# Chunk 0 of the first batch in halves of the heads, query chunk 2 behind the first products, w1 ahead of w2

## The chip, the cores and the metric

The kernel runs on one core of a Trainium2 chip. The metric is the device time of one execution in microseconds (us), of which the median of several runs is taken. Five engines work at once, each through its own list of instructions in order: PE (TensorE: matrix products and transposes; its weight loads are shown apart as PEld), DVE (VectorE), ACT (ScalarE), POOL (GpSimd) and SP (SyncE), the last two here mostly to issue transfers. PE writes to PSUM, an accumulation memory that DVE and ACT read; everything else lies in SBUF.

## What is computed

A linear attention with cosine weights feeds a multiplicative feed-forward layer. There are 8 batches of 8 heads, 576 positions and 64 features:

```
r = relu(x);  phi(x) = [r * cos(theta), r * sin(theta)]          # 128 features, for q and k
kv = phi(k)^T @ v;   z = sum over positions of phi(k)
attn = (phi(q) @ kv) / (phi(q) @ z + 1e-6)
x = attn as (4608 tokens, 512)
out = ((x @ w1) * (x @ w2)) @ w3 @ w_out                          # w1, w2: 512 x 1024
```

The kernel computes `w3 @ w_out` once and applies it as one matrix, `w34b`. It works in bf16, with sums in fp32.

## The kernel before, in words

**Tiles and stages.** The positions of a batch are cut into five chunks, four of 128 and one of 64. For each chunk `features` writes phi of q or k: the cosine half on DVE (L264), the sine half on ACT (L268), with a DVE variant (L271) for four heads of the very first chunk. `kv_first` (for batch 0) and `kv_chunk` (for the others) sum kv and z on PE. `q_tr` and `q_tr_halves` transpose phi(q) of a chunk on PE, one 128x128 transpose for each of the 8 heads, into a PSUM tile `pst`, and copy it to `qpT` (L344 in two halves with two PSUM tiles, L332 on DVE or L333 on ACT as one copy). `num` (L359) makes 8 products of 65 columns for a chunk, numerator and denominator, into a two-bank PSUM tile, four heads in each bank. Its `normalize` adds 1e-6 to the denominators (L375), inverts them (L376) and multiplies (L377) into the block `xblk`. `x_tr` transposes that block with four PE transposes (L411) into a `pst` tile and copies them to `xT` (L413), 512 tokens wide.

The feed-forward layer runs over 9 tiles of 512 tokens (`ffn_groups`). For tile 0, with four chunks that come one after another, the first products (L456) are made in pieces: half a tile, and of that quarters of 128 tokens, so that they can begin when chunk 0 is there. `multiply` copies x @ w1 out of PSUM on ACT (L461) and multiplies on DVE (L462). The products with `w34b` come last (L526).

**What sets the order.** The order is written out by hand (`manual_schedule`): every engine gets its instructions in the order in which the Python code calls them, and waits by semaphores that the framework sets. What depends on what in PSUM is tracked by bank: a second access to a bank from another engine waits for the first, also where the columns differ. `ffn_groups` is a generator that yields between groups of products, and the main loop calls at each yield what `at(slot, ...)` has put there, so attention work stands between the products. `pst` tiles come from the pool `ps_tr` with two buffers, taken in turn: the third tile can be written when the copies of the first have ended.

**Around the change.** Before the loop, the start-up is written out: kv of batch 0, the features and transposes of query chunks 0 to 2, `num(0, 0)`, the marker that releases further loads on POOL (`other_loads`, which waits for `xblk` of chunk 0), the features of chunk 3, `x_tr(0, 0)`, `num(0, 1)`, and the transposes of query chunk 2 with their ACT copy. `idle_mms` are products of zeros that no one reads. Slot 1, behind the first quarter of products, holds `x_tr(0, 1)`, the transposes of query chunk 3 and `num(0, 2)`. Slot 3 holds `x_tr(0, 2)` and `num(0, 3)`.

In the first quarter of tile 0 the products alternate between the two weights:

```
for quarter in range(2):
    for i in range(2):
        for ps, w in ((a, w1b), (b, w2b)):
            products(ps[:, ds(256 * i + 128 * quarter, 128)], w, i, ...)
        if half == 0 and quarter == 0 and i == 0:
            yield
```

The first yield is slot 0, which is empty before the change.

Of the kernel before, what the change touches and what calls it, by code (L numbers as in the profile page):

```python
# [11 lines left out]
BF16 = mybir.dt.bfloat16  # L12
I32 = mybir.dt.int32
ALU = mybir.AluOpType
ACTF = mybir.ActivationFunctionType

P = 128
H, S, D = 8, 576, 64
# [5 lines left out]
def columns_of(b, c):  # L24


    if b % 2 == 0:
        return 128 * c
    return 0 if c == 4 else 64 + 128 * c
# [39 lines left out]
def kernel(  # L69
# [11 lines left out]
    nc = tc.nc  # L81
# [53 lines left out]
    w1b = const.tile([P, 4, DFF], BF16, name="w1b")  # L135
    w2b = const.tile([P, 4, DFF], BF16, name="w2b")
# [108 lines left out]
    feat = {}  # L245
# [8 lines left out]
    def att_of(b):  # L254
        if b not in att:
            att[b] = {"qpT": phi.tile([P, H, S], BF16, name="qpT"), "x": {}}
        return att[b]

    def features(b, dst, src, c, cos=True, sin=True, scalar_heads=H):

        R = ROWS[c]
        at = c if b == 0 else NCH + c
        if cos:
            nc.vector.tensor_scalar(out=dst[:R, c, :, 0:D], in0=src[:R, :, c, :], scalar1=0.0,  # L264
                                    scalar2=cosv[:R, at:at + 1], op0=ALU.max, op1=ALU.mult)
        if sin:
            n = scalar_heads
            nc.scalar.activation(out=dst[:R, c, 0:n, D:F], in_=src[:R, 0:n, c, :], func=ACTF.Relu,  # L268
                                 scale=sinv[:R, at:at + 1], bias=0.0)
            if n < H:  # L270
                nc.vector.tensor_scalar(out=dst[:R, c, n:H, D:F], in0=src[:R, n:H, c, :],  # L271
                                        scalar1=0.0, scalar2=sinv[:R, at:at + 1],
                                        op0=ALU.max, op1=ALU.mult)
# [51 lines left out]
    def q_tr(b, c, evac=True):  # L325
        R = ROWS[c]
        qp = feat[b][1]
        pst = ps_tr.tile([P, 8, 128], BF16, name="pst")
        for h in range(H):
            nc.tensor.transpose(pst[:, h, :], qp[:, c, h, :], identb[:])  # L330
        dst, src = att_of(b)["qpT"][:, :, ds(columns_of(b, c), R)], pst[:, :, 0:R]
        on_vector = lambda: nc.vector.tensor_copy(out=dst, in_=src)  # L332
        on_scalar = lambda: nc.scalar.copy(out=dst, in_=src)  # L333
        if evac:
            on_vector()
        return on_vector, on_scalar

    def q_tr_halves(b, c):

        for half in range(2):  # L340
            pst = ps_tr.tile([P, 8, 128], BF16, name="pst")
            for i in range(4):
                nc.tensor.transpose(pst[:, i, :], feat[b][1][:, c, 4 * half + i, :], identb[:])
            nc.vector.tensor_copy(out=att_of(b)["qpT"][:, ts(half, 4), ds(columns_of(b, c), 128)],  # L344
                                  in_=pst[:, 0:4, :])

    def num(b, c, chain=True, in_two=False):
        rows = out_rows(b, c)
        R = ROWS[c]
        at = columns_of(b, c) - rows.start  # L350
        qpT, kvs = att[b]["qpT"], att[b]["kvs"]
        if b == 0 and c == 0:
            nt = ps_first.tile([P, 2, 512], FP32, name="pfirst")
        else:
            pool = more_att[0] if more_att and order_of(b).index(c) % 2 == 0 else ps_att
            nt = None if in_two else pool.tile([P, 2, 512], FP32, name="pnum")
        banks = [ffn_tile(), ffn_tile()] if in_two else [nt[:, g, :] for g in range(2)]
        for h in range(H):
            nc.tensor.matmul(banks[h // 4][:, ds((h % 4) * 65, 65)], lhsT=qpT[:, h, ds(at, 128)],  # L359
                             rhs=kvs[:, h, :], start=True, stop=True)  # L360
        if b < 2:
            rows, R = slice(0, P), P
        if in_two:
            parts = [(slice(g, g + 1), t[rows, 0:260].rearrange("p (g h e) -> p g h e", g=1, e=65))
                     for g, t in enumerate(banks)]
        else:
            parts = [(slice(0, 2), nt[rows, :, 0:260].rearrange("p g (h e) -> p g h e", e=65))]
        xblk = sm.tile([P, 2, 4, D], BF16, name="xblk", bufs=4)
        att[b]["x"][c] = xblk

        def normalize():
            den = sm.tile([P, 2, 4], FP32, name="den")
            for g, n4 in parts:
                G = g.stop - g.start
                nc.vector.tensor_scalar_add(out=den[rows, g], in0=n4[:, :, :, 64], scalar1=1e-6)  # L375
                nc.vector.reciprocal(out=den[rows, g], in_=den[rows, g])  # L376
                nc.vector.tensor_tensor(out=xblk[rows, g], in0=n4[:, :, :, 0:D],  # L377
                                        in1=den[rows, g].unsqueeze(3).to_broadcast([R, G, 4, D]),
                                        op=ALU.mult)

        if chain:
            normalize()
        return normalize
# [9 lines left out]
    xT = {}  # L393

    def x_tr(b, c, by_vector=False):
        R, rows = ROWS[c], out_rows(b, c)
        xblk = att[b]["x"].pop(c)
        xf = xblk[:].rearrange("p g h d -> p (g h d)")
        if b % 2 == 0:
            slot = S * b + 128 * c  # L400
        else:
            slot = S * b + (0 if c == 4 else 64 + 128 * c)
        t, o = divmod(slot, 512)
        if t not in xT:
            xT[t] = xtp.tile([P, 4, 512], BF16, name="xT")
        if b >= 2 or (b, c) in ((0, 4), (1, 3)):
            nc.sync.dma_start_transpose(out=xT[t][:, :, ds(o, R)], in_=xf[rows])
            return
        pst = ps_tr.tile([P, 8, 128], BF16, name="pst")
        for kc in range(4):  # L410
            nc.tensor.transpose(pst[:, kc, :], xf[:, ts(kc, 128)], identb[:])  # L411
        copy = nc.vector.tensor_copy if by_vector else nc.scalar.copy
        copy(out=xT[t][:, :, ds(o, R)], in_=pst[:, 0:4, rows])  # L413
# [36 lines left out]
    def ffn_groups(t):  # L450
# [15 lines left out]
        def on_half(half):  # L466

            if half == 1 and t == 0:
                banks = [(ffn_tile(), ffn_tile()) for _ in range(2)]
                for quarter in range(2):  # L470
                    for pair, (a, b) in enumerate(banks):
                        for i in range(2):
                            for ps, w in ((a, w1b), (b, w2b)):
                                products(ps[:, ds(256 * i + 128 * quarter, 128)], w, 2 * pair + i,
                                         ds(256 + 128 * quarter, 128))
                        if quarter == 1:
                            multiply(a, b, pair, half)
                        if quarter == 0 or pair == 1:
                            yield
                return  # L480
            for pair in range(2):
                a, b = ffn_tile(), ffn_tile()
                if pair == 0 and t == 0:
                    for quarter in range(2):
                        for i in range(2):
                            for ps, w in ((a, w1b), (b, w2b)):
                                products(ps[:, ds(256 * i + 128 * quarter, 128)], w, i,
                                         ds(256 * half + 128 * quarter, 128))
                            if half == 0 and quarter == 0 and i == 0:
                                yield  # L490
                        if quarter == 0:
                            yield
                else:
                    for ps, w in ((a, w1b), (b, w2b)):
                        for i in range(2):
                            products(ps[:, ts(i, 256)], w, 2 * pair + i, ts(half, 256))
                        if w is w1b and (t == 1 or half == 0):
                            yield
                multiply(a, b, pair, half)
                yield  # L500
# [52 lines left out]
    def at(s, *calls):  # L553
        slots[s] += calls
# [42 lines left out]
    num(0, 0)  # L597
    q_tr(0, 1, evac=False)[1]()
    other_loads(att[0]["x"][0][:, 0, 0, 0:1])
    features(0, q0f, q0, 3, sin=False)  # L600
    features(0, q0f, q0, 3, cos=False)
    idle_mms(2)
    x_tr(0, 0, by_vector=True)
    num(0, 1)
    q_tr(0, 2, evac=False)[1]()
    ps_ffn = []
    for stack in first:
        stack.close()
# [2 lines left out]
                                                     space=bass.MemoryType.PSUM)))  # L611


    at(1, lambda: x_tr(0, 1, by_vector=True), lambda: q_tr(0, 3, evac=False)[1](), lambda: num(0, 2))
    at(3, lambda: x_tr(0, 2), lambda: num(0, 3))
    at(5, lambda: x_tr(0, 3))
# [74 lines left out]
```

## Time and profile before

| what | value |
|---|---|
| median of 5 runs | 249.3 us (249.09 to 249.71) |
| the profiled execution, its own time | 249.5 us |
| span of its profile | 247.7 us |
| granted TensorE clock, mean | 0.996 |
| busy: PE, DVE, ACT, POOL | 97%, 55%, 53%, 38% of the span |
| first products of tile 0 (L456) | 16.11 us |
| first products of its second quarter | 18.08 us |

The profile shows one execution. Its parts are the busy time of each engine, who waited for whom, the chain of work that ended last (followed back from the last instruction), and the timeline: one row for each group of equal instructions with its start, its duration, engine, line, operation, output and inputs, and, in brackets, the idle time of its engine before it and what ended that. Starts count from the beginning of the span. Matmuls overlap: the next starts before the one before has ended, so PE's pace is read from the starts.

### The profile page before, as it was taken

The page shows a single profiled execution, that of the slowest core. Times are in us where ns is not written, and L with a number is a line of the kernel's source. Part 1 is how long each engine was busy: PE and PEld are TensorE (multiplying, and loading weights), DVE is VectorE, ACT ScalarE, POOL GpSimd, SP SyncE. Part 2 cuts the span into 40 slices and gives each one's busy share as a digit, 9 for nine tenths or more (in the row PEclk, how much of TensorE's full clock was granted, in tenths as well). Part 3 has the DMA queues.
Part 4 walks back from the last instruction along what each step waited for, and adds up shares of the span by engine and source line. Part 5 has one row for each costly group of instructions (what it writes and reads, how often), then busy time and mean ns, then how long its engine had stood idle before and what let it go on. Part 6 is the DMA issues. An engine that isn't in the chain of part 4 may idle for free.

```text
span 247.7 us, 5041 instructions
## 1 busy us (share of the span) xinstructions
PE 241.5 (97%) x1872; PEld 130.4 (53%) x1872; DVE 136.5 (55%) x336; ACT 130.4 (53%) x266; POOL 93.2 (38%) x196
## 2 busy tenths in 40 slices
PE   8999999999999999999999999999999999999993
PEld 2479545566965445455544555455545544444442
DVE  7875652668967445656665575557554643403320
ACT  2676323767933973476448655754585234334322
POOL 7655342124412361217122622352231006969600
PEclk9999999999999999999999999999999999999998
DMA  6999999999989979999999999999995428898925
GB/s 196 177 194 199 201 207 205 198 185 174 155 141 154 163 117 152 126 142 95 170 175 166 128 159 149 173 155 112 170 124 111 88 42 247 263 292 276 294 51 127
DMA packets 84745, 41.22 MB, mean 166 GB/s; under 512 B 52337, under 2 KB 81265, under 8 KB 84721
## 3 DMA queue, kind: packets, MB, share of 16 engines
q0 software_dynamic: 35472, 27.20, 72.0%
q1 hardware_dynamic: 49088, 13.57, 36.4%
q8 instruction: 14, 0.23, 0.4%
q10 hardware_dynamic: 160, 0.13, 0.2%
q14 instruction: 11, 0.08, 0.1%
HBM read 38.80 MB, written 9.44 MB: 195 GB/s over the span
## 4 chain that ended last, share of the span: by engine, by line
PE 92%; DMA 3%; DVE 1%; issue 1%; POOL 1%; ACT 0%; ACTq 0%; POOLq 0%
PE ffnps L456 50%; PE ffnps L526 24%; PE ffnps L231 6%; PE pnum L359 4%; PE pnum L299 4%; DMA qs<-in_q_dram 3%; PE pst L219 1%; PE pst L330 1%; PE pst L411 1%; POOL vs L127 0%; PE ffnps L542 0%; ACT osb L544 0%; DVE xblk L377 0%; PE pfirst L359 0%; ACTq L441 0%
## 5 line engine op out<-in xcount | busy, mean ns | idle before, releaser
L456 PE MATMUL ffnps<-xT,w2b 128*128 128x512 bf16 (+2 forms) x344 | 75.5, 344 | 0.0
L456 PE MATMUL ffnps<-xT,w1b 128*128 128x512 bf16 (+2 forms) x344 | 75.5, 344 | 0.0
L513 DVE TENSOR_TENSOR abT<-asb,ffnps 128x512 bf16<-128x512 bf16 x64 | 43.9, 687 | 53.9 <-PE ffnps L456 52.0
L526 PE MATMUL ffnps<-w34b,abT 128*128 128x512 bf16 x280 | 65.0, 379 | 0.0
L509 ACT CAST asb<-ffnps 128x512 bf16<-128x512 f32 x64 | 37.4, 585 | 50.0 <-PE ffnps L456 45.2
L456 PEld LDWEIGHTS <-w2b 128*128 128x128 bf16 x344 | 31.0, 98 | 27.3
L456 PEld LDWEIGHTS <-w1b 128*128 128x128 bf16 x344 | 30.6, 98 | 26.1 <-issue 0.6
L561 POOL COPY seen<-mark 1x1 bf16<-1x1 bf16 x50 | 8.9, 177 | 85.9 <-ACT mark L559 85.8
L526 PEld LDWEIGHTS <-abT 128*128 128x128 bf16 x280 | 26.0, 98 | 27.9 <-DVE abT L513 0.2
L533 ACT COPY osb<-ffnps 128x512 f32<-128x512 f32 x35 | 20.5, 585 | 34.9 <-PE ffnps L526 34.8
L268 ACT ACTIVATE qp<-qs,sinv 128x512 bf16<-128x512 bf16 (+2 forms) x40 | 28.1, 714 | 2.0 <-DMA qs<-in_q_dram 2.0
L377 DVE TENSOR_TENSOR xblk<-pnum,den 128x512 bf16<-128x512 f32 (+1 forms) x37 | 25.6, 691 | 1.3
L291 POOL COPY va<-vs 128x512 bf16<-128x512 bf16 (+1 forms) x30 | 18.0, 631 | 21.5 <-DMA vs<-in_v_dram 21.1
L268 ACT ACTIVATE kp<-ks,sinv 128x512 bf16<-128x512 bf16 (+1 forms) x35 | 25.0, 718 | 1.0 <-DMA ks<-in_k_dram 1.0
L441 POOL DMA_DIRECT2D out_dram<-osb x42 | 22.1, 531 | 2.5 <-issue 2.1
L359 PEld LDWEIGHTS <-qpT 128*128 128x128 bf16 x320 | 15.4, 98 | 8.7 <-DVE qpT L344 0.6
L375 DVE TENSOR_SCALAR den<-pnum 128x8 f32<-128x8 f32 (+1 forms) x37 | 6.1, 164 | 22.6 <-PE pnum L359 22.5
L231 PE MATMUL ffnps<-woutb,w3T 128*128 128x512 bf16 x64 | 15.8, 380 | 0.0
L359 PE MATMUL pnum<-kvs,qpT 128*128 128x65 bf16 x296 | 15.8, 194 | 0.0
L264 DVE TENSOR_SCALAR qp<-qs,cosv 128x512 bf16<-128x512 bf16 (+1 forms) x40 | 15.3, 391 | 0.7 <-DMA qs<-in_q_dram 0.7
L299 PEld LDWEIGHTS <-kp 128*128 128x128 bf16 x280 | 11.4, 98 | 4.1
L264 DVE TENSOR_SCALAR kp<-ks,cosv 128x512 bf16<-128x512 bf16 (+1 forms) x35 | 12.9, 377 | 0.0
(86 smaller groups left out, 182.4 us busy)
## 6 DMA issues: line engine op xcount, KB each, us to landing
out_dram<-osb POOLq DMA_DIRECT2D x16, 256.0 KB, 4.5
out_dram<-osb POOLq DMA_DIRECT2D x24, 128.0 KB, 3.7
qs<-in_q_dram POOLq DMA_DIRECT2D x9, 256.0 KB, 7.3
ks<-in_k_dram POOLq DMA_DIRECT2D x7, 320.0 KB, 5.9
qs<-in_q_dram POOLq DMA_DIRECT2D x7, 320.0 KB, 6.1
vs<-in_v_dram POOLq DMA_DIRECT2D x7, 320.0 KB, 5.7
ks<-in_k_dram POOLq DMA_DIRECT2D x7, 256.0 KB, 7.0
vs<-in_v_dram POOLq DMA_DIRECT2D x7, 256.0 KB, 5.1
```

The costliest lines, as they stand in the source:

```text
L231: nc.tensor.matmul(acc[:, :], lhsT=w3T[:, lc, :], rhs=woutb[:, lc, :], start=(lc == 0), stop=(lc == 7))
L264: nc.vector.tensor_scalar(out=dst[:R, c, :, 0:D], in0=src[:R, :, c, :], scalar1=0.0, scalar2=cosv[:R, at:at + 1], op0=ALU.max, op1=ALU.mult)
L268: nc.scalar.activation(out=dst[:R, c, 0:n, D:F], in_=src[:R, 0:n, c, :], func=ACTF.Relu, scale=sinv[:R, at:at + 1], bias=0.0)
L299: nc.tensor.matmul(kvt[:, h // 4, ds((h % 4) * 65, 65)], lhsT=kp[:, c, h, :], rhs=va[:, c, h, 0:D + 1], start=(i == 0 and h % 4 == 0), sto ...
L359: nc.tensor.matmul(banks[h // 4][:, ds((h % 4) * 65, 65)], lhsT=qpT[:, h, ds(at, 128)], rhs=kvs[:, h, :], start=True, stop=True)
L377: nc.vector.tensor_tensor(out=xblk[rows, g], in0=n4[:, :, :, 0:D], in1=den[rows, g].unsqueeze(3).to_broadcast([R, G, 4, D]), op=ALU.mult)
L441: on.dma_start(out=rows[:, :, cols], in_=osb[64 * i:64 * i + rows.shape[0], :, cols])
L456: nc.tensor.matmul(out, lhsT=w[:, kc, ts(jc, 128)], rhs=x[:, kc, tok], start=(kc == 0), stop=(kc == 3))
L509: nc.scalar.copy(out=asb[:], in_=aT[:, :])
L513: nc.vector.tensor_mul(out=abT[:, jc, :], in0=asb[:], in1=bT[:, :])
L526: nc.tensor.matmul(ops[:, :], lhsT=abT[:, jc, ts(ms, 128)], rhs=w34b[:, jc, :], start=(jc == 0), stop=(jc == 7))
L533: nc.scalar.copy(out=osb[:, ms % 2, :], in_=ops[:, :])
```

## The change

Four things change, all in the start-up of batch 0 and in tile 0.

1. For chunk (0, 0), `normalize` multiplies in two halves of four heads, and `x_tr` makes two transposes and one copy of 128x256 for each half, both copies on DVE. One `pst` tile holds both halves.
2. The cosine features of chunk 3 on DVE are called behind `x_tr(0, 0)` instead of ahead of it; the sine features on ACT stay ahead.
3. The transposes of query chunk 2 move from ahead of the loop to slot 0. The new `q_tr_two` copies four heads on ACT and four on DVE, from one `pst` tile.
4. In the first pair of tile 0's half, the w1 products of both column groups come ahead of the w2 products, and slot 0 lies between them.

```
+    def q_tr_two(b, c):
+        pst = ps_tr.tile([P, 8, 128], BF16, name="pst")
+        for h in range(H):
+            nc.tensor.transpose(pst[:, h, :], feat[b][1][:, c, h, :], identb[:])
+        dst = att_of(b)["qpT"][:, :, ds(columns_of(b, c), 128)]
+        nc.scalar.copy(out=dst[:, 0:4], in_=pst[:, 0:4, :])
+        nc.vector.tensor_copy(out=dst[:, 4:8], in_=pst[:, 4:8, :])
...
-                nc.vector.tensor_tensor(out=xblk[rows, g], in0=n4[:, :, :, 0:D],
-                                        in1=den[rows, g].unsqueeze(3).to_broadcast([R, G, 4, D]),
-                                        op=ALU.mult)
+                for i in (range(G) if (b, c) == (0, 0) else [slice(0, G)]):
+                    i = slice(i, i + 1) if isinstance(i, int) else i
+                    part = slice(g.start + i.start, g.start + i.stop)
+                    nc.vector.tensor_tensor(
+                        out=xblk[rows, part], in0=n4[:, i, :, 0:D],
+                        in1=den[rows, part].unsqueeze(3).to_broadcast([R, i.stop - i.start, 4, D]),
+                        op=ALU.mult)
...
         pst = ps_tr.tile([P, 8, 128], BF16, name="pst")
+        if (b, c) == (0, 0):
+            for half in range(2):
+                for kc in range(2 * half, 2 * half + 2):
+                    nc.tensor.transpose(pst[:, kc, :], xf[:, ts(kc, 128)], identb[:])
+                nc.vector.tensor_copy(out=xT[t][:, ts(half, 2), ds(o, R)], in_=pst[:, ts(half, 2), rows])
+            return
...
                     for quarter in range(2):
-                        for i in range(2):
-                            for ps, w in ((a, w1b), (b, w2b)):
+                        for ps, w in ((a, w1b), (b, w2b)):
+                            for i in range(2):
                                 products(ps[:, ds(256 * i + 128 * quarter, 128)], w, i,
                                          ds(256 * half + 128 * quarter, 128))
-                            if half == 0 and quarter == 0 and i == 0:
+                            if half == 0 and quarter == 0 and w is w1b:
                                 yield
...
-    features(0, q0f, q0, 3, sin=False)
     features(0, q0f, q0, 3, cos=False)
     idle_mms(2)
-    x_tr(0, 0, by_vector=True)
+    x_tr(0, 0)
+    features(0, q0f, q0, 3, sin=False)
     num(0, 1)
-    q_tr(0, 2, evac=False)[1]()
...
+    at(0, lambda: q_tr_two(0, 2))
     at(1, lambda: x_tr(0, 1, by_vector=True), lambda: q_tr(0, 3, evac=False)[1](), lambda: num(0, 2))
```

## The prediction

> **What bounds the kernel now.** I read the page's first two parts, then who TensorE (PE) waited for, then the chain that ended last, and then the timeline of 14 to 18 us. Line numbers are those of the kernel before.
>
> From the page, the busy times:
>
> ```profile
> PE 241.5 (97%) x1872; PEld 130.4 (53%) x1872; DVE 136.5 (55%) x336; ACT 130.4 (53%) x266; POOL 93.2 (38%) x196
> ```
>
> Everything that the matrix engine waited for, over the whole span (total us, times, longest):
>
> ```profile
> PE unread L180 <- DVE zeros L156: 1.2, 1, 1.2
> PE pst L411 <- DVE xblk L377: 0.3, 1, 0.3
> PE pst L343 <- DVE qp L271: 0.3, 1, 0.3
> ```
>
> The reader is to see that PE is the bound, and that its last recorded idle time ends at 15.07 us, where the transposes of chunk 0 (L411) wait for the normalized block (L377). Behind it PE has work queued to 243 us, and waits for nothing that is tied to an absolute time, such as a load. So whatever the change gains or loses before the steady stream begins moves the whole rest and appears once, undiminished, in the time. The change touches 14 to 19 us alone, so the question is when the work behind it starts.
>
> The chain of waits in the window from 0 to 32 us (start, us, what):
>
> ```profile
> 14.32 0.70 DVE xblk L377
> ...
> 15.07 0.40 PE pst L411 x4
> 15.47 0.36 PE pnum L359 x8
> 15.83 0.45 PE pst L330 x8
> 16.28 0.89 PE ffnps L456 x16
> 17.17 0.28 PE pst L411 x4
> 17.45 0.53 PE pst L330 x8
> 17.98 0.26 PE pnum L359 x8
> 18.24 1.77 PE ffnps L456 x24
> ```
>
> From the timeline of 14 to 18 us (start, us, engine, line), the rows that the sum uses:
>
> ```profile
> 14.33 1.01 ACT L333 COPY qpT<-pst 128x1024 bf16<-128x1024 bf16 x1 [0.32 <-PE pst L330]
> ...
> 15.50 0.42 DVE L413 COPY xT<-pst 128x512 bf16<-128x512 bf16 x1 [0.23 <-PE pst L411]
> ...
> 15.87 0.17 DVE L375 TENSOR_SCALAR den<-pnum 128x8 f32<-128x8 f32 x1
> ...
> 16.31 0.69 DVE L377 TENSOR_TENSOR xblk<-pnum,den 128x512 bf16<-128x512 f32 x1
> 16.32 1.01 ACT L333 COPY qpT<-pst 128x1024 bf16<-128x1024 bf16 x1 [0.35 <-PE pst L330]
> ...
> 17.38 0.61 PE L330 MATMUL pst<-identb,qp 128*128 128x128 bf16 x8
> ...
> 18.08 0.39 PE L456 MATMUL ffnps<-xT,w1b 128*128 128x128 bf16 x4
> ```
>
> Two small waits are left in that stretch. The second L411 group issues at 17.06, 0.05 after chunk 1's block ends (16.31 + 0.69 = 17.00). The transposes of query chunk 3 issue at 17.38 and not at 17.28, because their PSUM buffer is that of query chunk 2, whose ScalarE (ACT) copy ends at 16.32 + 1.01 = 17.33. My mark is the row at 18.08, the first products of the second quarter: from there PE runs without a wait.
>
> **Prices.** From the starts of successive rows: a 128-column PE instruction issues every 0.055 us (L411 to L359 at 17.06, 17.38: 8 transposes 0.44, 8 products 0.45), a 65-column one every 0.033 (8 take 0.26), and a transpose ends 0.22 after it starts, so a pair takes 0.28. A signal needs 0.05 from VectorE (DVE) to PE (15.01 to 15.06), 0.03 from PE to DVE (15.47 to 15.50), 0.04 from PE to ACT, 0.03 from ACT to DVE (19.59 to 19.62). From the groups of DVE and then of ACT, kept apart by shape (mean ns in the last column but one):
>
> ```profile
> L377 DVE TENSOR_TENSOR xblk<-ffnps,den 128x256 bf16<-128x256 f32 x4 | 1.7, 424 | 0.1
> ...
> L221 DVE COPY w3T<-pst 128x1024 bf16<-128x1024 bf16 x8 | 5.5, 691 | 9.1 <-PE pst L219 9.1
> ...
> L413 ACT COPY xT<-pst 128x512 bf16<-128x512 bf16 x4 | 2.3, 576 | 1.9 <-PE pst L411 1.9
> ```
>
> A 128x256 DVE copy out of PSUM has no row. The 128x512 copy takes 0.42 and the 128x1024 one 0.69, so 256 elements cost 0.135 beside a fixed 0.15: 0.285. Bounds are 0.15 and 0.42.
>
> **Part 1: chunk 0 in halves.** The two normalize halves take 0.42 each, the second starting about 0.08 before the first ends (as L264 at 14.93 does behind L377): 14.32 to 14.74 and 14.66 to 15.08. So the first pair of transposes can issue at 14.79 instead of 15.07, a gain of 0.28. But both pairs write one PSUM tile, in one bank, and in the built program the second pair waits not only for the second half of the block but also for DVE's copy of the first pair. That makes a ladder: pair 14.79 to 15.07; copy 15.10 to 15.39; second pair 15.44 to 15.71; copy 15.74 to 16.02; PE hears of it at 16.07. Queued behind the waiting pair, in order, stand the 8 products of num(0,1) (their query columns are ready at 15.34 from ACT, so they could start at 15.39): they now issue from 15.55 to 15.82. Then come the first w1 products, of which two need only the first half of xT; the third waits until 16.07, and the other six issue by 16.41. Before, 16 products started at 16.11. The bounds on the copy shift 16.07 by -0.27 and +0.27.
>
> The cosine features of chunk 3 (L264) ran at 14.93 in DVE's idle time. They now stand behind the two xT copies, at about 15.94, and ahead of den(0,1), which starts at 16.22 and not at 15.87. Chunk 1's block is then ready at about 17.36 and its transposes issue at about 17.41 instead of 17.06. GpSimd's marker for the further loads waits for the first half alone and moves 0.27 earlier; no product waits for those loads, so I count nothing. SP gets no changed order.
>
> **Part 2: query chunk 2.** Its 8 transposes leave their place before the first products and go behind the w1 ones: issued 16.41 to 16.85, the last ending at 17.01. (Before: 15.67 to 16.28.) In the built program the DVE copy of heads 4 to 7 waits for ACT's copy of heads 0 to 3, since both read one bank. ACT: 17.05 to 17.63 (0.58). DVE: 17.66 to 18.08 (0.42). One ACT copy of both took 1.01, so the split saves nothing: 0.58 + 0.03 + 0.42 = 1.03. Behind that stand the transposes of query chunk 3, which need the same buffer: 18.08 + 0.05 = 18.13 instead of 17.38.
>
> The Trainium skill ("PSUM — Partial Sum Buffer", section "PSUM bank collisions raise a hardware error") says that two engines must be kept from one bank and quadrant at the same time, reads against reads included, so this order is a necessity and not a choice of the scheduler; by a sum without it, the two copies would lie side by side, 0.36 us earlier.
>
> **Part 3: w1 ahead of w2.** It is the same 16 products in another order, 0.45 per eight. Inside the first quarter it only gives the place for part 2. In the second quarter it lets ACT's first multiply copy (L461) start earlier, off PE's path. Cost 0, covered by PE's own queue; without that cover it could be worth 0.45 either way.
>
> **Sum.** PE's w2 products run from 16.85 to 17.30, chunk 1's transposes 17.41 to 17.63, then idle until 18.13; query chunk 3 to 18.57, num(0,2) to 18.83, and the second quarter begins at 18.83 instead of 18.08: **+0.75 us**. DVE's copy of chunk 1's xT (18.00 to 18.42) and all behind it are in time for that. Against the profiled execution's 249.5 us (span 247.7) this gives 250.25; the median of the five runs is 249.3, 0.2 lower, so for a median I say **250.1**.
>
> **Rivals.**
> A. Only one of the two bank waits costs its price. Without the wait of the second pair, num(0,1) starts at 15.39, w1 at 15.66, chunk 2's transposes end at 16.71, ACT ends at 17.33, DVE at 17.78: query chunk 3 at 17.83, +0.45. Without the wait between the copies, DVE's copy runs behind chunk 1's block, 17.30 to 17.72, ACT's to 17.63: 17.77, +0.39. In time: 249.7 to 249.75. For it: PE and DVE starts can be off by some hundredths. Against: both waits stand in the built program.
> B. Not slower: early start pays. If neither wait costs anything, chunk 3's transposes issue at 17.4 to 17.5, +0.1. If the ladder ends early enough (w1 products begun by 15.6, both copies of chunk 2 done before 17.2), PE loses all its idle time between 14.72 and 18.08: 0.35 before 15.07, 0.05 and 0.11 behind it, about 0.5: 248.8. The decision point is the end of chunk 2's copies against 17.33; I find it at 18.08, so 0.75 would have to be missing.
> C. More idle time lowers the granted clock. The row for 14.10 to 15.07 shows PE 0.62 us busy of 0.97 at a clock of 1.00, and only 240.0 to 247.7, with 4.1 us idle, shows 0.88. My gaps are 0.37 and 0.32. If one came all the same, the stretch of 3.4 us to 18.1 at half speed would add as much again: up to 253.5.
> D. The change does not do what it says: the order in the built program is that of the text, so only its waits decide, which is A and B.
>
> **How the numbers follow.** Chances: forecast 74%, its own range +0.5 to +1.0 by the copy's bounds (249.8 to 250.3); A 14%; B 8%, of which half is a real gain; C 4%. The range from 249.6 to 250.6 takes in A and a longer ladder, and leaves out B and C. Two kernels can be told apart from about 0.2%, 0.5 us. Faster by more: 4%, from B. Within: the rest of B and most of A, 16%. Slower by more: the forecast, some of A, and C, 80%.
>
> **What would show it.** In the profile after: the first transposes of chunk 0 at 14.8 (part 1's gain); the second pair near 15.44 and its copy ending near 16.0 (the ladder); den(0,1) near 16.2; ACT and DVE copies of chunk 2 one behind the other, ending near 18.1; a PE wait of about 0.3 to 0.5 before query chunk 3; the second quarter at 18.8. I am wrong if chunk 2's copies overlap, if half copies take much less than 0.28, or if PE has a wait further on that swallows the shift.

## The result, and the profile after

The changed kernel takes longer: median **250.62 us** over 54 runs (249.96 to 252.27), against 249.69 over 94 runs of the kernel before (249.09 to 252.31). The ratio is 1.0039, 95% interval 1.0031 to 1.0047, which is +0.97 us (0.77 to 1.17). The profiled execution took 250.12 us with a span of 248.3, against 249.5 and 247.7.

The loss is in the stretch that the change touches. Line numbers after the change: products L474 (before L456), transposes of chunk 0 in pairs L425 with their copies L426, those of the other chunks L429 and L431, `q_tr_two` L341 (transposes), L343 (ACT), L344 (DVE), `num` L367, normalize L383, L384, L388. In the experiments some of them shift by a line or two; with two tiles (e8, e3) `q_tr_two` has its transposes in L343 and both copies in L344. In both traces the loads of this execution come at slightly different times: q landed 0.44 us earlier after the change. So I do not compare bare starts, but count from one event that lies ahead of all the edits: DVE's start on the denominators of chunk 0, at 13.88 us before and 13.44 us after. To the first products of the second quarter it is 18.08 - 13.88 = 4.20 us before and 18.46 - 13.44 = 5.02 us after: **+0.82**. From there to the end of the span it is 229.62 and 229.84 (the spans are given to a tenth, so these two are good to 0.05).

Everything that PE waited for after the change (total us, times, longest):

```profile
PE unread L180 <- DVE zeros L156: 1.2, 1, 1.2
PE pst L425 <- DVE xT L426: 0.4, 1, 0.4
PE pst L429 <- DVE xblk L388: 0.2, 1, 0.2
PE pst L351 <- DVE qp L271: 0.2, 1, 0.2
```

The wait of 0.3 for the whole block of chunk 0 is gone. In its place stand a wait of 0.4 of the second pair of transposes for the copy of the first, and one of 0.2 of chunk 1's transposes for their block (the first and the last row lie ahead of the change). The list is not complete, though: it leaves out waits that the chain shows. The chain of what ended last, after the change, in the stretch (start, us, what):

```profile
13.88 0.43 DVE xblk L388
...
14.36 0.30 PE pst L425 x2
...
14.68 0.30 DVE xT L426
...
15.03 0.27 PE pst L425 x2
15.30 0.26 PE pnum L367 x8
15.56 0.11 PE ffnps L474 x2
...
16.17 0.46 PE pst L341 x8
...
16.66 0.59 ACT qpT L343
...
17.28 0.44 DVE qpT L344
...
17.75 0.61 PE pst L330 x8
18.36 0.26 PE pnum L367 x8
18.62 1.77 PE ffnps L474 x24
```

Before the change this chain ran on PE alone from 15.07 on. Now it leaves PE twice. From 14.68 to 15.03 it is DVE's half copy, on which the second pair waits. From 16.66 to 17.75 it is ACT's and then DVE's copy of query chunk 2, on which query chunk 3 waits.

The timeline after the change holds one row that the prediction had wrong, the second:

```profile
15.33 0.75 POOL L190 DMA_DIRECT2D w1b<-in_moe_w_dram  x1
...
15.54 0.66 DVE L264 TENSOR_SCALAR qp<-qs,cosv 128x512 bf16<-128x512 bf16 x1
...
16.54 0.69 DVE L388 TENSOR_TENSOR xblk<-pnum,den 128x512 bf16<-128x512 f32 x1
```

The cosine features of chunk 3 take 0.66 us and not 0.34, so the block of chunk 1 ends at 16.54 + 0.69 = 17.23. ACT's copy ends at 16.66 + 0.59 = 17.25. DVE's copy of query chunk 2 needs both, and they come within 0.02 us of each other: two paths of equal length lead to the same instruction. That is why the experiments below must take things away one at a time and together.

### The profile page after: what moved, and what is told of

The parts are those of the page before. It is cut to its first block, busy times and chain, and to the rows that moved or that the text cites. A ratio compares the mean times of both kernels' runs of the same rounds, so it can differ in the third digit from the quotient of the medians.

```text
span 248.3 us, 5044 instructions
## 1 busy us (share of the span) xinstructions
PE 241.8 (97%) x1872; PEld 130.5 (53%) x1872; DVE 138.4 (56%) x339; ACT 129.9 (52%) x266; POOL 93.2 (38%) x196
## 4 chain that ended last, share of the span: by engine, by line
PE 87%; DMA 7%; DVE 2%; issue 1%; POOL 1%; ACT 1%; ACTq 0%; POOLq 0%; SPq 0%; DVEq 0%
PE ffnps L474 47%; PE ffnps L544 24%; PE ffnps L231 6%; PE pnum L367 4%; DMA qpT<-qp 4%; DMA qs<-in_q_dram 3%; PE pnum L299 3%; PE pst L219 1%; PE pst L330 1%; DVE qp L264 1%; PE pst L429 1%; POOL vs L127 0%; PE ffnps L560 0%; ACT osb L562 0%; DVE abT L531 0%
## 5 line engine op out<-in xcount | busy, mean ns | idle before, releaser
L474 PE MATMUL ffnps<-xT,w1b 128*128 128x512 bf16 (+2 forms) x344 | 75.3, 344 | 0.0
L474 PE MATMUL ffnps<-xT,w2b 128*128 128x512 bf16 (+2 forms) x344 | 75.2, 344 | 0.0
L474 PEld LDWEIGHTS <-w2b 128*128 128x128 bf16 x344 | 30.9, 98 | 27.3
L474 PEld LDWEIGHTS <-w1b 128*128 128x128 bf16 x344 | 30.6, 98 | 26.1 <-issue 0.3
L388 DVE TENSOR_TENSOR xblk<-pnum,den 128x512 bf16<-128x512 f32 (+1 forms) x37 | 25.6, 691 | 1.5 <-DVE den L384 0.2
L367 PEld LDWEIGHTS <-qpT 128*128 128x128 bf16 x320 | 15.4, 98 | 8.9 <-DMA qpT<-qp 0.6
L383 DVE TENSOR_SCALAR den<-pnum 128x8 f32<-128x8 f32 (+1 forms) x37 | 6.0, 163 | 23.0 <-PE pnum L367 22.8
L264 DVE TENSOR_SCALAR qp<-qs,cosv 128x512 bf16<-128x512 bf16 (+1 forms) x40 | 17.4, 444 | 0.6 <-DMA qs<-in_q_dram 0.6
L367 PE MATMUL pnum<-kvs,qpT 128*128 128x65 bf16 x296 | 15.8, 194 | 0.1
L264 DVE TENSOR_SCALAR kp<-ks,cosv 128x512 bf16<-128x512 bf16 (+1 forms) x35 | 12.3, 360 | 0.1
```

The source lines that it names most:

```text
L388: nc.vector.tensor_tensor(out=xblk[rows, part], in0=n4[:, i, :, 0:D], in1=den[rows, part].unsqueeze(3).to_broadcast([R, i.stop - i.start, ...
L474: nc.tensor.matmul(out, lhsT=w[:, kc, ts(jc, 128)], rhs=x[:, kc, tok], start=(kc == 0), stop=(kc == 3))
```

## Experiments

Parts 1, 2 and 3 are those of the prediction: chunk 0 in halves with the features moved; query chunk 2 in slot 0; w1 ahead of w2.

**Theory A**: the copies of query chunk 2, one behind the other because they read one PSUM bank, set the end. **Theory B**: the ladder in part 1 (pair, copy, pair, copy) is the whole loss. **Theory C**: the copies' path and DVE's path (ladder, slow features, block of chunk 1) are nearly equally long, so that removing one leaves the other, and the prices do not add.

Each experiment was timed in five rounds. With so few rounds the interval of a ratio is about 0.002 wide to each side (0.5 us), so the stretch in the trace is what tells them apart. It is one execution each, but a steady one: the changed kernel again gave 5.02, and an edit that should not touch it gave 4.20 again. "Against before" is the stretch less 4.20; "L264" is the duration of the cosine features; "rest" is the span behind the stretch, good to 0.05.

| run | stretch, us | against before | L264 | rest | time ratio, 95% |
|---|---|---|---|---|---|
| before | 4.20 | 0 | 0.34 | 229.62 | |
| changed | 5.02 | +0.82 | 0.66 | 229.84 | 1.0039 (1.0031 to 1.0047) |
| e0 changed, again | 5.02 | +0.82 | 0.66 | 229.80 | 1.0023 (1.0005 to 1.0042) |
| e2 no halves | 4.99 | +0.79 | 0.34 | 229.69 | 1.0030 (1.0006 to 1.0054) |
| e8 no halves, two tiles | 4.53 | +0.33 | 0.34 | 229.77 | 1.0013 (0.9989 to 1.0037) |
| e3 two tiles | 4.88 | +0.68 | 0.66 | 229.57 | 1.0038 (1.0013 to 1.0063) |
| e4 ladder off | 4.80 | +0.60 | 0.34 | 229.89 | 1.0038 (1.0019 to 1.0057) |
| e5 both waits off | 4.36 | +0.16 | 0.35 | 229.71 | 1.0005 (0.9983 to 1.0027) |
| e11 two tiles, loads later | 4.57 | +0.37 | 0.34 | 231.54 | 1.0089 (1.0060 to 1.0119) |
| e1 query chunk 2 in its old place | 4.79 | +0.59 | 0.66 | 230.53 | 1.0026 (1.0003 to 1.0050) |
| e7 features moved only | 4.34 | +0.14 | 0.34 | 229.75 | 0.9992 (0.9970 to 1.0014) |
| e6 w1 first only | 4.20 | 0 | 0.34 | 231.23 | 0.9998 (0.9983 to 1.0014) |
| e12 idle time filled | 4.11 | -0.09 | 0.34 | 231.97 | 1.0004 (0.9981 to 1.0026) |

### e2: part 1 undone

The changed kernel with whole normalize, whole transposes and one copy, and the features of chunk 3 back in their place; parts 2 and 3 stay.

```
-                for i in (range(G) if (b, c) == (0, 0) else [slice(0, G)]):
+                for i in [slice(0, G)]:
...
-        if (b, c) == (0, 0):
+        if False:
...
+    features(0, q0f, q0, 3, sin=False)
     features(0, q0f, q0, 3, cos=False)
     idle_mms(2)
-    x_tr(0, 0)
-    features(0, q0f, q0, 3, sin=False)
+    x_tr(0, 0, by_vector=True)
```

> Chunk 0 is normalized, transposed and copied whole again, and the cosine features of chunk 3 stand in their old place; query chunk 2 in slot 0 and w1 ahead of w2 stay. I read the stretch from DVE's first query features to the first products of the second quarter: 6.35 us before, 7.17 us after (+0.82). Theory A (the copies of query chunk 2, one behind the other, behind the w1 products set the end): the w1 products start at xT's copy, 0.1 earlier than the ladder let them finish, so the chain ends where it did: stretch +0.75 to +0.85 over before, time about as the changed kernel (+0.9). Theory B (part 1, the ladder in one PSUM bank and the moved features, is what costs): stretch +0.3 or less.

Measured: +0.79. Without any ladder nearly the whole loss remains, so theory B falls. The chain of e2 (start, us, what):

```profile
16.52 0.46 PE pst L341 x8
...
17.01 0.59 ACT qpT L343
...
17.62 0.43 DVE qpT L344
...
18.10 0.61 PE pst L330 x8
```

It runs through the two copies, although DVE was free well before: its block of chunk 1 was done at 16.24 + 0.69 = 16.93.

### e8: part 1 undone, and two PSUM tiles for query chunk 2

As e2, and `q_tr_two` uses a tile, and so a bank, for each half (the lines that these replace are left out):

```
+        for half, copy in enumerate((nc.scalar.copy, nc.vector.tensor_copy)):
+            pst = ps_tr.tile([P, 8, 128], BF16, name="pst")
+            for i in range(4):
+                nc.tensor.transpose(pst[:, i, :], feat[b][1][:, c, 4 * half + i, :], identb[:])
+            copy(out=dst[:, ts(half, 4)], in_=pst[:, 0:4, :])
```

> As the run without halves, but query chunk 2 is transposed into two PSUM tiles of four heads, so ACT's copy and DVE's copy may lie side by side. Theory A: ACT's copy ends 0.4 earlier and DVE's no longer waits for it; query chunk 3 then waits only for buffers free at about 17.5 in the numbers of before: stretch +0.3 to +0.4 over before, 0.45 less than without this edit. Theory A fails if the stretch stays at +0.75 or more. Theory B: no change against the run without halves.

Measured: +0.33, so taking away the wait between the copies is worth 0.79 - 0.33 = **0.46** here. The timeline of e8:

```profile
16.56 0.58 ACT L344 COPY qpT<-pst 128x512 bf16<-128x512 bf16 x1 [0.89 <-PE pst L343]
...
16.59 0.61 PE L474 MATMUL ffnps<-xT,w2b 128*128 128x128 bf16 x8
...
16.79 0.42 DVE L344 COPY qpT<-pst 128x512 bf16<-128x512 bf16 x1
...
17.20 0.38 PE L429 MATMUL pst<-identb,xblk 128*128 128x128 bf16 x4
...
17.42 0.61 PE L330 MATMUL pst<-identb,qp 128*128 128x128 bf16 x8
```

The copies now lie side by side and end at 17.14 and 17.21, and query chunk 3 waits for neither. The 0.33 that is left has two other sources. Before the change, PE transposed query chunk 2 (15.67 to 16.11) while DVE copied xT of chunk 0 (15.50 to 15.92). With these transposes moved away, PE finishes num(0,1) at 15.37 in e8 and has nothing to do until xT is there: its first w1 product starts at 15.70, an idle time of 0.33. The move itself uncovers a copy that had been hidden.

The second source comes with the edit: two tiles take both `pst` buffers, so chunk 1's transposes must have the one that ACT is reading. The w2 products, eight at 0.055, have been issued by 16.59 + 0.44 = 17.03, and chunk 1's block was done at 16.71. Its transposes issue at 17.20, 0.06 behind the end of ACT's copy: 0.17 of idle time, which no wait list shows. That the buffer is the reason is inferred from these times, and e5 repeats it. In exchange the two small waits of before (0.05 and 0.11) are gone: 0.33 + 0.17 - 0.16 = 0.34, which accounts for the 0.33. So 0.46 is what the edit gains net of the 0.17 that it costs.

### e3: two PSUM tiles in the changed kernel

The edit of `q_tr_two` shown for e8, alone.

> The changed kernel with query chunk 2 in two PSUM tiles, halves of chunk 0 kept. Bare theory A: ACT's copy no longer holds DVE's back, stretch about 0.3 to 0.4 shorter than the changed kernel's, +0.45 over before. Theory C (two paths of equal length: the doubled features instruction makes chunk 1's block end at the same time at which ACT's copy ends, so DVE can't copy earlier in any case): stretch unchanged, +0.75 to +0.85 over before.

Measured: +0.68. The same edit that was worth 0.46 in e8 is worth 0.14 here. The timeline of e3:

```profile
16.75 0.69 DVE L388 TENSOR_TENSOR xblk<-pnum,den 128x512 bf16<-128x512 f32 x1
...
17.36 0.41 DVE L344 COPY qpT<-pst 128x512 bf16<-128x512 bf16 x1
...
17.83 0.61 PE L330 MATMUL pst<-identb,qp 128*128 128x128 bf16 x8
```

The copies are free of each other, but DVE comes to its copy only at 17.36, since the features took 0.66 and the block of chunk 1 is late; chunk 1's transposes, which stand ahead of query chunk 3 on PE, wait for that block. The result lies in neither expected range: well above theory A's +0.45, but below theory C's +0.75 to +0.85. What is gained is that DVE begins its copy 0.08 before its block ends, and not 0.03 after ACT's copy (3.71 behind the origin in place of 3.84). Theory A alone cannot say this; theory C can, once that hand-over is counted.

### e4: the ladder alone taken away

The second pair of chunk 0 goes into another bank, that of the tile `kva`, so that it does not wait for the copy of the first pair. `q_tr_two` keeps its one tile.

```
             for half in range(2):
+                if half == 1:
+                    pst = ps_idle.tile([P, 8, 128], BF16, name="kva")
                 for kc in range(2 * half, 2 * half + 2):
```

> The changed kernel with only the ladder taken away: the second pair of chunk 0's transposes goes into the bank that kv's sum has left; query chunk 2 keeps its one tile and its two copies one behind the other. With both waits off the moved features instruction started before GpSimd's descriptor writing and took 0.35, and chunk 1's block was early. So what is left is the chain of the two copies alone: query chunk 3 about 0.45 later than with both waits off, stretch +0.6 over before. If the copies' order were worth only the 0.14 by which two tiles alone shortened the changed kernel: +0.3.

Measured: +0.60. DVE's path is shorter (no ladder, and the features take 0.34 in this run), and the copies' path is left, as the timeline of e4 shows:

```profile
16.91 0.59 ACT L343 COPY qpT<-pst 128x512 bf16<-128x512 bf16 x1 [0.93 <-PE pst L341]
...
17.53 0.42 DVE L344 COPY qpT<-pst 128x512 bf16<-128x512 bf16 x1 [0.46 <-ACT qpT L343]
...
18.01 0.49 PE L330 MATMUL pst<-identb,qp 128*128 128x128 bf16 x6 [0.46 <-DVE qpT L344]
```

The brackets name the wait outright: DVE idle for 0.46 until ACT's copy ended, PE idle for 0.46 until DVE's ended. In the changed kernel the DVE row had no bracket, because the late block filled DVE's time up to the same moment. The first w1 products start at 15.82 here, behind the second copy; in the changed kernel two of them start ahead of it, so this edit has a small cost of its own.

### e5: both bank waits taken away

The edits of e3 and e4 together.

> The changed kernel with both bank waits taken away: the second pair of chunk 0's transposes goes into the bank that kv's sum has left, and query chunk 2 into two PSUM tiles. The second pair then waits for its half of the block alone (15.13 instead of 15.44 in the numbers of before). Features instruction 0.34: chunk 1's block as early as before, stretch +0.1. Features instruction 0.66: +0.4. If the ladder cost nothing beside DVE's path: +0.68, as with two tiles alone. In no case below 0.

Measured: +0.16, and a time that cannot be told from before. So e4 less e5 is 0.44, what two tiles gain once DVE is early, which agrees with 0.46 from e8. Of the change as it was meant to be, nothing is gained even so: with both waits gone it is not ahead of the kernel before. The timeline of e5 shows where most of the 0.16 may lie:

```profile
15.91 0.69 DVE L388 TENSOR_TENSOR xblk<-pnum,den 128x512 bf16<-128x512 f32 x1
...
16.22 0.59 ACT L344 COPY qpT<-pst 128x512 bf16<-128x512 bf16 x1 [0.71 <-PE pst L343]
16.25 0.61 PE L476 MATMUL ffnps<-xT,w2b 128*128 128x128 bf16 x8
...
16.86 0.38 PE L431 MATMUL pst<-identb,xblk 128*128 128x128 bf16 x4
```

It is the wait for the buffer again. The w2 products have been issued by 16.25 + 0.44 = 16.69 and the block is done at 16.60, but chunk 1's transposes issue at 16.86, 0.05 behind the end of ACT's copy: 0.17. With a third buffer the change might come out about even with before; that is an estimate, and no run here has one.

### e11: two tiles, and the marker for the loads later

As e3, and POOL's marker waits for the block of chunk 1 and not for chunk 0's, so that POOL issues no load while DVE makes the features.

```
-    other_loads(att[0]["x"][0][:, 0, 0, 0:1])
     features(0, q0f, q0, 3, cos=False)
     idle_mms(2)
     x_tr(0, 0)
     features(0, q0f, q0, 3, sin=False)
     num(0, 1)
+    other_loads(att[0]["x"][1][:, 0, 0, 0:1])
```

> The changed kernel with query chunk 2 in two PSUM tiles (alone: +0.68) and with GpSimd's marker behind chunk 1's block instead of chunk 0's, so that no descriptors are written while the moved features instruction runs; the loads behind it come some 2.5 us later. If GpSimd's descriptor writing is what doubled that instruction: it takes 0.34, chunk 1's block is 0.3 earlier, stretch +0.35 to +0.45. If something else (its place behind the PSUM copies) doubled it: 0.66 again and +0.68.

Measured: +0.37 in the stretch, 0.31 less than e3. The timeline of e11 has the features at their usual length, with POOL silent until 17.34:

```profile
15.90 0.34 DVE L264 TENSOR_SCALAR qp<-qs,cosv 128x512 bf16<-128x512 bf16 x1
...
17.34 0.19 POOL L201 COPY seen<-xblk 128x1 bf16<-128x1 bf16 x1 [5.81 <-DVE xblk L388]
```

So it was POOL's loads that lengthened them. As a kernel e11 is worse, 1.0089: PE now waits for the weights that come later (PE's waits of e11):

```profile
PE ffnps L231 <- DMA woutb<-in_moe_w_out_dram: 0.8, 1, 0.8
PE pst L219 <- DMA w3b<-in_moe_w_dram: 0.6, 1, 0.6
```

What is left of the ladder is about e11 less e5: 0.21.

### e1: query chunk 2 back in its old place

The changed kernel without `q_tr_two`: the transposes of chunk 2 ahead of the products, with one ACT copy.

```
     num(0, 1)
+    q_tr(0, 2, evac=False)[1]()
...
-    at(0, lambda: q_tr_two(0, 2))
```

> The changed kernel with query chunk 2 back in its old place and with its one ACT copy; halves of chunk 0, moved features and w1 ahead of w2 stay. The stretch from the denominators of chunk 0 to the first products of the second quarter is 4.20 us before, 5.02 in the changed kernel (+0.82). ACT's copy then ends at about 17.5 in the numbers of before and no longer decides; DVE's path does (moved features, chunk 1's block). Features instruction 0.66 as in the changed kernel: chunk 1's transposes as late as there, stretch +0.5 to +0.6. Features instruction 0.34: +0.25. Bare theory B (part 1 is the whole loss): +0.8.

Measured: +0.59. No copies in series are left, and the rest of the change still costs most of the loss, by DVE's path: features 0.66 from 15.99, block of chunk 1 done at 16.98 + 0.69 = 17.67, its transposes at 17.73 (timeline of e1):

```profile
15.78 0.75 POOL L190 DMA_DIRECT2D w1b<-in_moe_w_dram  x1
...
15.99 0.66 DVE L264 TENSOR_SCALAR qp<-qs,cosv 128x512 bf16<-128x512 bf16 x1
...
16.98 0.69 DVE L388 TENSOR_TENSOR xblk<-pnum,den 128x512 bf16<-128x512 f32 x1
...
17.73 0.40 PE L429 MATMUL pst<-identb,xblk 128*128 128x128 bf16 x4 [0.39 <-DVE xblk L388]
```

Each path by itself is thus worth 0.59 (e1) or 0.79 (e2), and both together 0.82. That is theory C's signature.

### e7: the features moved, alone

The kernel before, with the cosine features of chunk 3 called behind `x_tr(0, 0, by_vector=True)`.

> The kernel before, with only the cosine features of chunk 3 on DVE moved behind x_tr(0, 0). In the changed kernel this instruction took 0.66 us instead of 0.34, beside a GpSimd descriptor write (15.33 to 16.08). If it does so here: chunk 1's block is late by about 0.55 us and the stretch grows by about 0.44. If it takes 0.34: +0.12. If DVE's order did not matter (theory A in its bare form): 0.

Measured: +0.14 in the stretch, nothing that the time can tell. The features take 0.34 there, though a load is being issued (timeline of e7):

```profile
15.34 0.74 POOL L202 DMA_DIRECT2D w2b<-in_moe_w_dram  x1
...
15.87 0.34 DVE L264 TENSOR_SCALAR qp<-qs,cosv 128x512 bf16<-128x512 bf16 x1
```

### e6: w1 first, alone

The kernel before, with the loops over `i` and over the weights exchanged, as in part 3.

> The kernel before with only the w1 products ahead of the w2 products in the first pair of tile 0, slot 0 left empty. The same 16 products issue in the same 0.9 us and nothing on PE waits for their order: stretch 0 (within 0.03), time 0. Rival: ACT's copy of the first sum starts 0.2 to 0.4 earlier and something behind it gains: stretch 0, but the rest of the run up to 0.2 shorter.

Measured: stretch 4.20, unchanged; ratio 0.9998 (0.9983 to 1.0014). Part 3 costs and gains nothing by itself. (The rest of this one execution is 1.6 us longer, of which a PE wait for ACT near 134 us makes 1.1; its twelve runs do not show that in their median.)

### e12: a version meant to beat both

The kernel before, with the transposes of query chunk 2 in PE's idle time ahead of chunk 0's (in place of `idle_mms`), and chunk 0's transposes in the bank of `kva`, so that they need not wait for a `pst` buffer (the cut shows the first of the two).

```
-    idle_mms(2)
+    q_tr(0, 2, evac=False)[1]()
     x_tr(0, 0, by_vector=True)
     num(0, 1)
-    q_tr(0, 2, evac=False)[1]()
```

> The kernel before, with the 8 transposes of query chunk 2 in place of the two idle products ahead of chunk 0's transposes (0.44 us of work into 0.94 us of idle products and idle time), and chunk 0's transposes in the bank that kv's sum has left, since both buffers are taken. PE then waits for chunk 1's block at 17.05 as before, but the transposes of query chunk 3 need not wait for ACT: stretch -0.1, the rest being held by DVE's chain; time -0.1 us, below what a time can show. If PE's work after 15.07 set the end: -0.4.

Measured: -0.09 in the stretch; time ratio 1.0004 (0.9981 to 1.0026). With the transposes gone from there, PE has issued num(0,1) by 15.43 + 0.26 = 15.69, and the products wait for xT of chunk 0 until 16.02 (0.33). Then PE has nothing from 16.90 until chunk 1's block lets its transposes start at 17.09 (0.19). These 0.52 us stand in place of the 0.16 of small waits before, so most of the 0.45 us of PE work that was moved comes back as idle time. No version here beats the kernel before by what can be measured.

### e0: the changed kernel again

No edit, to see how well the stretch repeats.

> The changed kernel again, for a second trace. Stretch +0.82 as in the first trace (the descriptor writing and the features instruction meet in the same place, since both hang on chunk 0's block); time about 0.9 over before. What is behind the stretch differs from execution to execution: between 229.57 and 229.84 us in five traces, 230.5 and 232.0 in two. If the changed kernel lost more there of itself, this trace too would lie above the 229.62 of before by 0.2 or more.

Measured: 5.02 again, features 0.66 again, ratio 1.0023 (1.0005 to 1.0042).

## Why the prediction was right or wrong, point by point

**The direction and the mechanism were right.** Counted from the start on chunk 0's denominators, the predicted and measured steps of the forecast are: first pair 0.91 and 0.92; second pair 1.56 and 1.59; third w1 product 2.19 and 2.24; transposes of chunk 2 2.53 and 2.57; ACT's copy 3.17 and 3.22; DVE's copy 3.78 and 3.84; query chunk 3 4.25 and 4.31; second quarter 4.95 and 5.02. The error grows from 0.01 to 0.07, by at most 0.02 from one step to the next. The sum said +0.75 and the stretch gave +0.82.

**The half copy**, which had no row, was put at 0.285 and measured 0.29.

**The step that failed in part 1** was the term "at about 15.94, and ahead of den(0,1)" with the features at 0.34: they took 0.66, and the block of chunk 1 came 3.79 after the origin and not 3.48. By luck it cost nothing beyond the sum, because ACT's copy ended 0.02 later than that block: the idle time that I put ahead of query chunk 3 (0.50) only moved in part ahead of chunk 1's transposes (17.29), and 0.24 was left (17.51 to 17.75). It decides, though, what each wait is worth. Linked to it is "I count nothing" for POOL's marker moving earlier. No product waited for those loads, as said, but DVE did. The prediction's own numbers held the meeting. In the timeline of before POOL's second issue is

```profile
16.04 0.75 POOL L190 DMA_DIRECT2D w1b<-in_moe_w_dram  x1
```

Moved 0.27 earlier it starts at 15.77, and the features were put at 15.94, inside it. And the trace of before shows what such a meeting can cost (the rows at 116 us in the last section).

**Rival A's prices were too low.** Without the second pair's wait I had +0.45, and e4 gave +0.60, because its w1 products stood behind the second copy. Without the wait between the copies I had +0.39; e3 gave +0.68 because of the slow features, and e11, with the loads out of the way, gave +0.37. Rival B's "neither wait costs" was +0.1 and measured +0.16 (e5); its real gain of 0.5 did not show in any run. Rival C did not come: the granted clock over the stretch was 1.00. Rival D did not come either: the order is that of the text. That the two copies must not read one bank at the same time, which part 2 gives as the reason for their order, is untested: in every run here they read one bank one behind the other, or two banks.

**Part 3** at 0 was right (e6).

**The step that failed in the number** is the last one, "the median of the five runs is 249.3, 0.2 lower, so for a median I say 250.1". The five runs were low ones: of 94 runs of the kernel before, the lowest quarter ends at 249.42, and the median is 249.69, which is 0.39 above the baseline that I used. With 249.69 + 0.75 the forecast would have been 250.44, and 250.51 with the measured stretch. So of the 0.52 that the median lies above the forecast, 0.39 is the baseline, 0.07 the stretch, and the rest (0.11 less 0.05 of rounding) has no shown source. The measured 250.62 lies 0.02 above the stated range, whose width came from the copies' bounds and had no term for the baseline. Why the five were low stays open. It need not be chance alone: in the three sets of runs that went with the experiments, the kernel before has medians of 249.68, 249.92 and 250.09.

**What stays open.** The measured +0.97 (0.77 to 1.17) takes in the 0.82 of the stretch, so nothing more need exist; whether another tenth arises behind the stretch can't be settled with these runs. The rest is 229.84 and 229.80 in the two traces of the changed kernel, and 229.57 to 229.89 in those experiments that have no late PE wait. The traces of e6 and e12 are 1.6 and 2.4 us longer there; a PE wait for ACT near 134 us makes 1.1 and 1.2 of that, and its cause I did not find.

## What to carry to other kernels

Splitting a PSUM tile's work over two engines saves nothing while both halves lie in one bank: take a tile for each half, and look whether the second consumer is free at all and whether the pool has a buffer left for whatever comes next. When work is moved on a busy engine, look up what it had been covering: here the moved transposes had hidden a copy, and the move uncovered 0.33 us of idle time. When work is moved in time, look also at what other engines issue at its new place. Where two paths end within hundredths of each other, price edits together as well as singly, and take the baseline from as many runs as there are.

## What the hardware showed that I had not expected

The cosine features (a bf16 multiply from SBUF to SBUF on DVE) take 0.34 us, but 0.66 when they start 0.21 us after POOL begins the row of a load's issue (L190, 0.75 us long). This came in all four runs with that timing (the changed kernel twice, e3, e1), and each time the features ended 0.87 us after that row's start, as if they had been held until 0.53 us into it. They keep their 0.34 or 0.35 when they start 0.53 us into such a row (e7), when they start 0.11 us ahead of it (e4, e5) and when POOL issues nothing (e11). So it is not the whole row that blocks, and not the DVE instruction that came first.

This is not peculiar to the change. The kernel before has such meetings later in its span, where they need not cost time (timeline of before):

```profile
61.26 0.75 POOL L121 DMA_DIRECT2D qs<-in_q_dram  x1 [0.63 <-DMA vs<-in_v_dram]
...
61.39 0.34 DVE L264 TENSOR_SCALAR kp<-ks,cosv 128x512 bf16<-128x512 bf16 x1
...
116.30 0.68 POOL L121 DMA_DIRECT2D ks<-in_k_dram  x1 [0.16 <-issue]
116.58 0.49 DVE L264 TENSOR_SCALAR qp<-qs,cosv 128x512 bf16<-128x512 bf16 x1
```

Started 0.13 us into an issue, the features take 0.34; started 0.28 into one, 0.49. In the thirteen traces together (rows of this line and shape beside a load's issue, with no POOL copy beside them), all 35 that start ahead of the issue or at most 0.171 us into it take 0.34 to 0.36. Of the 61 that start 0.174 to 0.442 into it, 60 take 0.44 to 0.66. The 8 that start 0.53 or more into it take 0.34 to 0.35 again.

The Trainium skill ("SBUF — State Buffer", section "Who interferes with whom") says that DVE, in its two-port modes, and GpSimd share a pair of ports under an exclusive lock that goes to whoever issues first, and holds for that whole instruction. The traces agree in kind, since e4's features, which come first, are not slowed. They differ in extent: what blocks is only a part of the issue row, as the counts above show. That the features run in a two-port mode, and so that this lock is the cause, no run here shows.

ACT's and DVE's copies out of two different PSUM banks took 0.58 and 0.42 us side by side (e8), as long as each took alone.
